# Clustered attention and two MLPs: idle products taken out, long GpSimd passes split or moved, fp32r transposes, last chunk in halves, a new order

## The chip, the cores and the metric

The kernel runs on one core of a Trainium2 chip. Five engines work side by side, each through its own queue in order: TensorE (PE in the rows, its weight loads PEld), VectorE (DVE), ScalarE (ACT), GpSimd (POOL), and SyncE (SP), which issues nearly all transfers. The metric is the device time in microseconds of one execution, as a median of several; less is better. A row of a trace names an engine, a line of the kernel (L746), the tiles that are written and read, and times in microseconds from the start of the span, unless ns is written.

## The reference

Cut to what matters. q, k and v are [2, 8, 768, 64], the centroids [8, 16, 64]; the weights arrive as fp64.

```python
q_assign = np.argmax(np.einsum('bhsd,hcd->bhsc', q_n, c_n), axis=-1)   # q_n, k_n, c_n: unit length
k_assign = np.argmax(np.einsum('bhsd,hcd->bhsc', k_n, c_n), axis=-1)
mask = q_assign[:, :, :, None] == k_assign[:, :, None, :]
scores = np.where(mask, scale * np.matmul(q, k.transpose(0, 1, 3, 2)), -1e9)
attn = softmax(scores)                                    # written out in the reference
x = np.matmul(attn, v)  ->  [B * S, H * D] = [1536, 512]
h = (x @ w1) * (x @ w2) @ w3                              # d_ff 1024
x = h @ w_out                                             # [1536, 512]
h = x @ w_in                                              # d_ff 2048
out = (h * np.clip(h + 3.0, 0.0, 6.0) / 6.0) @ w_out2     # [1536, 512]
```

## The kernel before

Every operand of a product is held as two fp32r parts, a high one (H, h, hi) and a low one (L, l, lo), and a product is made of three: high by high, high by low, low by high. The weights come as pairs of 32-bit words and are put together on the chip in steps c0 to c5 (ScalarE c0 and c2, GpSimd or VectorE c1 at L1008, VectorE c3 at L1017 and c5 at L1021).

**Attention** runs over 16 heads (batch by head), each with 768 queries and keys in six blocks of 128. For each head: two loads (lq, lk) into one tile qkn, query beside key (L585); six transposes on TensorE in two runs of three (T, L608, id_f is the fp32 identity), a high part on ScalarE (qkh, L615) and a low part on VectorE (qkl, L618); the products with the centroids (pa, L647, two halves by high and low); nine small steps oh0 to oh8 (L661 to L677) from the products to a code of each row's cluster; copies and transfers of codes and parts into the operands kk, qkH and qkL (Dk, Dq, Ck, Cq). Then for each of 96 (head, block) pairs: scores (S1 and S, pst, L746, 512 and 256 columns), row maximum (mx, L758, VectorE), exponential (ex, L780, ScalarE) into p; transposes of p in runs of four on id_r, the fp32r identity (pT, L796), a high and a low part of these (ph, pl), and the product with v (av, L820). A tile of p is made readable as fp32r by writing one unused column of it (praw, the value three, L769 and L771): that write is op pw, on any of ScalarE, VectorE and GpSimd.

**The first MLP.** w3 @ w_out is computed first: w3 is transposed on TensorE, in 16 runs of four (wt, L1040, id_f), and multiplied with w_out (w_mm, psw, L1068). x @ w1 and x @ w2 are made batch by batch (psab, L1144 and L1396), their product is g, and g by the combined weights gives x of the second MLP. From some 350 us on, the second batch and then the whole **second MLP** (psh L1707, po L1751, about 457 us to the end) run by a scheme with seven products where blocks would need eight; the sums and differences of its operands are made on VectorE, ScalarE and GpSimd, and each has its low part as a subtraction (L421 on GpSimd through sub_pool, L424 on VectorE through sub_dve). Names: Ll, Wl, gsl, xwl are low parts of weights and states, xs and xsum are sums of states. The twelve output chunks of 128 rows by 512 columns are copied by ScalarE (out_copy, tile osb) and stored by SyncE (out_store, L1761).

**Idle products** (idle_pe, L530 to L534, ops in L568 to L573): six places with 4, 2, 3, 5, 4 and 3 products of 128 by 512 on the identity, whose result nobody reads.

**What sets the order.** Every step is an op of a plan with an engine (or a choice of them), what it needs and which buffers it takes and gives back. The table RANK gives each op its place in one list of some 4,000, and ON the engine where there is a choice; Plan.order only verifies both. The list is emitted in this order, so each engine's queue is that list cut down to its ops.

Of the kernel before, what the change touches and what calls it, by code (L numbers as in the profile page):

```python
# [54 lines left out]
    "T": """  # L55
        17 19 27 38 143 145 275 280 426 429 562 563 699 701 814 819 935 938 1062 1068 1180 1190 1317 1319 1451 1452 1579 1585 1717
        1721 1853 1869""",
    "qkh": """
        20 24 31 42 164 175 286 288 436 438 568 570 703 706 823 826 942 948 1069 1072 1195 1201 1320 1323 1454 1457 1589 1595 1725
        1739 1863 1873""",  # L60
    "qkl": """
        23 26 36 49 171 193 291 299 439 451 577 579 713 721 830 832 955 954 1078 1077 1200 1205 1324 1328 1466 1461 1592 1603 1732
        1744 1881 1883""",
# [3 lines left out]
    "Ck": """  # L67
        72 71 152 149 268 272 384 389 541 547 667 660 793 797 931 925 1048 1043 1154 1157 1296 1288 1414 1410 1555 1542 1696 1690 1841
        1836 1943 1950""",
    "Cq": """  # L70
        74 77 144 168 263 279 379 394 538 616 664 707 788 806 918 967 1055 1067 1146 1168 1301 1305 1420 1448 1553 1624 1692 1756 1846
        1896 1936 1956""",
# [123 lines left out]
    "xdone": "2215",  # L196
    "Wh": "2106 2126 2136 2176",
    "Wl": "2113 2135 2150 2182",
    "top": "2203",
    "gsh": "2208 2211 2214 2220 2229 2227 2245 2293",  # L200
    "gsl": "2212 2218 2222 2226 2240 2246 2304 2311",
    "x2": """
# [174 lines left out]
def cluster_attention_moe_kernel(  # L377
# [14 lines left out]
    nc = tc.nc  # L392
# [42 lines left out]
    def blk(i):  # L435
        return slice(i * 128, i * 128 + 128)
# [1422 lines left out]
```

## Time and profile before

| | |
|---|---|
| time, median of 3 runs | 741.15 us (740.86 to 741.38) |
| the profiled execution | 741.47 us |
| its span | 739.7 us |
| TensorE busy | 719.0 us, 97% of the span |
| VectorE busy | 611.5 us, 83% |
| ScalarE busy | 546.8 us, 74% |
| GpSimd busy | 201.9 us, 27% |

The busy share of TensorE is taken over the whole span: 0 to 36 us is a start in which it waits for loads and for other engines, and after that it hardly stops. Matmuls are pipelined, so the duration of one is longer than what it adds to the queue; what one costs is read from the start of one to the start of the next. A wait is charged to the instruction that stands behind it, with the engine and tile that ended it.

### The profile page before, as it was taken

How to read it: one execution, taken by the hardware profiler on the slowest of the kernel's cores; microseconds unless marked ns; L12 is line 12 of the kernel's file. 1: busy time of each engine (PE TensorE's matmuls, PEld its weight loads, DVE VectorE, ACT ScalarE, POOL GpSimd, SP SyncE). 2: the span in 40 equal slices, each digit the busy share in tenths (PEclk: the TensorE clock that was granted, in tenths of full speed). 3: DMA queues.
4: the chain of work that ended last, by engine and by line, in shares of the span. 5: the costliest groups of instructions: out<-in, count | busy, mean ns of one | idle time of the engine just before them, and what ended most of it. 6: DMA issues, size and time to landing. Idle time of an engine off the chain costs nothing. (4 is left out here: it accounts for less than half of the span.)

```text
span 739.7 us, 12102 instructions
## 1 busy us (share of the span) xinstructions
PE 719.0 (97%) x4143; PEld 661.4 (89%) x4143; DVE 611.5 (83%) x1060; ACT 546.8 (74%) x1043; POOL 201.9 (27%) x258
## 2 busy tenths in 40 slices
PE   5699999999999999999999999999999999999998
PEld 4488888888999999999999999999888998998986
DVE  6999999999899888778999999888897666666542
ACT  4899999898888878789867676676666656564543
POOL 3452646332635263355301110110110210011100
PEclk9999999999999999999999999999999999999999
DMA  8668555465563656453566752633222221411202
GB/s 237 157 167 221 152 150 162 114 161 140 150 185 119 182 155 170 115 156 114 178 200 228 238 175 100 220 122 138 91 86 85 72 72 60 137 61 58 72 28 86
DMA packets 81742, 101.97 MB, mean 138 GB/s; under 512 B 30960, under 2 KB 56592, under 8 KB 81680
## 3 DMA queue, kind: packets, MB, share of 16 engines
q1 hardware_dynamic: 81680, 101.20, 45.7%
q8 instruction: 33, 0.54, 0.3%
q14 instruction: 29, 0.24, 0.1%
HBM read 71.34 MB, written 15.78 MB: 118 GB/s over the span
## 5 line engine op out<-in xcount | busy, mean ns | idle before, releaser
L424 DVE TENSOR_TENSOR pl<-ptr,ph 128x512 fp32r<-128x512 f32 x144 | 96.3, 681 | 7.3 <-ACT ph L427 6.9
L758 DVE TENSOR_REDUCE den<-pst 128x1 f32<-128x768 f32 x96 | 91.1, 949 | 10.3 <-PE pst L746 9.2
L427 ACT ACTIVATE ph<-ptr 128x512 fp32r<-128x512 f32 x144 | 84.4, 597 | 14.0 <-PE ptr L796 9.7
L780 ACT ACTIVATE p<-pst,den 128x768 f32<-128x768 f32 x96 | 86.8, 904 | 8.8 <-DVE den L758 7.5
L1144 PE MATMUL psab<-xT,abhl 128*128 128x384 f32 x384 | 81.2, 343 | 0.6 <-DVE g L1154 0.6
L1008 POOL TENSOR_SCALAR cvt<-cvt 128x512 f32<-128x512 f32 x55 | 39.3, 718 | 142.0 <-ACT cvt L427 110.3
L746 PE MATMUL pst<-kk,qkL 128*128 128x512 f32 (+1 forms) x192 | 71.4, 374 | 4.8 <-ACT p L780 4.7
L1144 PEld LDWEIGHTS psab<-xT,abhl 128*128 128x128 f32 x384 | 65.4, 188 | 2.0 <-DVE g L1154 0.9
L820 PE MATMUL av<-ph,vs 128*128 128x384 f32 x192 | 66.4, 346 | 0.0
L796 PEld LDWEIGHTS ptr<-id_r,praw 128*128 128x128 f32 x576 | 60.9, 140 | 5.8 <-DVE pl L424 0.2
L746 PE MATMUL pst<-kk,qkH 128*128 128x512 f32 (+1 forms) x192 | 64.2, 338 | 1.7 <-ACT qkH L427 1.3
L820 PE MATMUL av<-pl,vs 128*128 128x384 f32 x192 | 64.8, 338 | 0.0
L427 ACT ACTIVATE m_sn<-psh 128x384 f32<-128x384 f32 x64 | 31.3, 489 | 44.3 <-PE psh L1707 43.4
L796 PE MATMUL ptr<-id_r,praw 128*128 128x128 f32 x576 | 63.6, 240 | 0.0
L427 ACT ACTIVATE cvt<-raw 128x512 f32<-128x512 f32 x72 | 48.1, 672 | 11.8 <-DVE cvs L1021 6.8
L1017 DVE SCALAR_TENSOR_TENSOR cvs<-cvt,cvs 128x512 int32<-128x512 int32 x72 | 50.0, 696 | 7.5 <-POOL cvt L1008 4.2
L1021 DVE SCALAR_TENSOR_TENSOR cvs<-cvt,cvs 128x512 int32<-128x512 int32 x72 | 50.8, 709 | 0.4
L427 ACT ACTIVATE cvs<-raw 128x512 int32<-128x512 uint8 x72 | 48.1, 670 | 1.8 <-DMA set<-cvs 1.8
L1068 PE MATMUL psw<-woh,wT 128*128 128x512 f32 x128 | 49.3, 405 | 0.0
L746 PEld LDWEIGHTS pst<-kk,qkL 128*128 128x128 f32 x192 | 36.0, 187 | 12.2 <-ACT p L780 9.9
L1751 PE MATMUL po<-m_whl,m_gv 128*128 128x512 f32 x162 | 44.0, 393 | 0.0
L1729 ACT ACTIVATE tt<-m_sn,three 128x384 f32<-128x384 f32 x48 | 29.4, 613 | 18.8 <-DVE m_sn L1717 9.0
(198 smaller groups left out, 1836.0 us busy)
## 6 DMA issues: line engine op xcount, KB each, us to landing
raw<-in_moe_w_dram SPq DMA_DIRECT2D x32, 512.0 KB, 4.3
m_gb<-set SPq DMA_DIRECT2D x64, 256.0 KB, 2.9
raw<-in_moe_w_out_dram SPq DMA_DIRECT2D x24, 512.0 KB, 3.4
raw<-in_moe_w_in_dram SPq DMA_DIRECT2D x16, 512.0 KB, 4.9
set<-cvs SPq DMA_DIRECT2D x32, 256.0 KB, 3.0
kk<-qkH SPq DMA_DIRECT2D x16, 384.0 KB, 4.0
abp<-cvs SPq DMA_DIRECT2D x16, 256.0 KB, 2.8
b_gv<-abp SPq DMA_DIRECT2D x16, 256.0 KB, 4.7
```

The lines of the kernel that those rows point to most:

```text
L424: nc.vector.tensor_tensor(out=out, in0=a, in1=b, op=ALU.subtract)
L427: nc.scalar.activation(out=out, in_=in_, func=AF.Copy, **kw)
L746: x = mm(out=psr[:, t, ks_], lhsT=TT[nm, h][:, i, cs_], rhs=flat(TT["K", h][:, a])[:, ks_], start=st, stop=sp)
L758: done["mx", n] = [other_banks(nc.vector.tensor_reduce(out=den_at(h, 0, c), in_=psS[h, c], axis=AX.X, op=ALU.max, negate=True), ("S", n + 1))]
L780: done["ex", n] = [other_banks(nc.scalar.activation(out=p, in_=psS.pop((h, c)), func=AF.Exp, bias=den_at(h, 0, c), accum_out=den_at(h, 1, ...
L796: x = nc.tensor.transpose(pt[:, blk(j)], raw[h, hf][0][:, c, blk(kb)], id_r)
L820: mm(out=t[:, 0:HF], lhsT=vs_t[h][:, 2 * s + i, :], rhs=x_[:, c0:c0 + HF], start=(s == 0 and i == 0 and n == 0), stop=(s == 2 and i == 1 a ...
L1017: stt(out=s, in0=cvt[key], scalar=3, in1=s, op0=ALU.logical_shift_left, op1=ALU.bitwise_or)
L1021: stt(out=s, in0=cvt.pop(key), scalar=-0x80000000, in1=s, op0=ALU.bitwise_and, op1=ALU.bitwise_or)
L1068: mm(out=ps, lhsT=wT[m, hf][:, a, blk(kk)], rhs=w_[hf][:, kk, :], start=(kk == 0 and n == 0), stop=(kk == 3 and n == 2))
L1144: mm(out=ps[:, 0:HF], lhsT=s[:, w, a, blk(kk)], rhs=xT0[0][:, x_, kk, hf * HF:hf * HF + HF], start=(kk == 0 and n == 0), stop=(kk == KD - ...
L1751: mm(out=outs[b, c], lhsT=g[:, a, blk(c % 3)], rhs=w[:, w_, :], start=(first and a == 0 and w_ == 0), stop=(last and a == 1))
```

## The change

1. The six ops with idle products and idle_pe go.
2. sub_pool splits a pass of 512 columns and more in two halves. The ops Ll, Wl, gsl, xsum and xwl are fixed on VectorE, and xs too where it was a choice: from GpSimd to VectorE go two of Wl (1024 columns), five of Ll (512), three of xs (768) and one of xwl (768).
3. The transposes of queries and keys of heads 1 to 15 (90) and those of w3 (64) are done on id_r. The tile is read as fp32r, for which one column more is written first: new ops tw (15, one a head) and ww (16, one a run), on VectorE 4 and 4, on ScalarE 3 and 4, on GpSimd 8 and 8. The tiles qkn and cvs have 8 columns more and their buffers are named one by one (slots), and the load of a head's queries stands behind the last transposes of the head two before.
4. The last output chunk is copied in two halves, columns 0 to 255 by ScalarE and 256 to 511 by VectorE, and stored in two halves of 128 KB, the first from ScalarE's queue and the second from SyncE's.
5. RANK and ON are new throughout. Of the choices that both kernels have, c1 goes from GpSimd to VectorE 13 times and back 8 times, wol2 from VectorE to GpSimd 8 times and back 6 times; xh two and woh one move between ScalarE and GpSimd, Ck one from ScalarE to VectorE.

```diff
-    "idle": "48 85 101 148 41 61",
-    "lq": "0 1 62 156 297 185 446 611 849 970 1052 1221 1163 1322 1545 1618",
+    "lq": "0 6 66 162 196 340 541 587 740 892 1125 1120 1218 1359 1501 1621",
...
     def sub_pool(out, a, b):
-        nc.gpsimd.tensor_tensor(out=out, in0=a, in1=b, op=ALU.subtract)
+        n = out.shape[-1] // 2 if out.shape[-1] >= 512 else out.shape[-1]
+        for i in range(0, out.shape[-1], n):
+            x = (slice(None),) * (len(out.shape) - 1) + (slice(i, i + n),)
+            nc.gpsimd.tensor_tensor(out=out[x], in0=a[x], in1=b[x], op=ALU.subtract)
...
-    op(("idle", 0), "pe", 0.0, lambda: idle_pe(4), ("id",), due=-30, take=("a",), drop=("a",))
...
+    def pad_write(e, pad):
+        if e == "act":
+            return nc.scalar.activation(out=pad, in_=three, func=AF.Copy)
+        return (nc.gpsimd if e == "pool" else nc.vector).tensor_copy(out=pad, in_=three)
...
+    def qk_raw(e, h):
+        del q_n[h]
+        x = ar.tile([128, S + 8], F32R, tag=f"qkn{h % 2}", name="qkr")
+        qraw[h] = x[:, 0:S].rearrange("p (c d) -> p c d", c=NC), pad_write(e, x[:, S:S + 1])
+
     def qk_T(h, hf):
+        if h:
+            x, w = qraw.pop(h) if hf else qraw[h]
+            pt = ps_s.tile([128, HF], F32R, tag="s", name="ptqk")
+            W_["st", h, hf] = pt.bitcast(F32)
+            for c in range(3):
+                i = nc.tensor.transpose(pt[:, blk(c)], x[:, 3 * hf + c, :], id_r)
+                tc.add_manual_dep(i.ins, w.ins.name, SYNC)
+            return
...
+    def w3_raw(e, m, hf):
+        del cvo["w3", m, hf]
+        x = base.tile([128, 520], F32R, tag=f"cvs{held['w3', m, hf]}", name="cvr")
+        wraw[m, hf] = x, pad_write(e, x[:, 512:513])
...
     def w3_T(m, hf):
-        pt = W_["pt", m, hf] = ps_s.tile([128, 4, 128], F32, tag="s", name="pt")
+        x, w = wraw.pop((m, hf))
+        pt = ps_s.tile([128, 4, 128], F32R, tag="s", name="pt")
+        W_["pt", m, hf] = pt.bitcast(F32)
         for i in range(4):
-            nc.tensor.transpose(pt[:, i, :], cvo["w3", m, hf][:, blk(i)], id_f)
-        cvo.pop(("w3", m, hf))
+            j = nc.tensor.transpose(pt[:, i, :], x[:, blk(i)], id_r)
+            tc.add_manual_dep(j.ins, w.ins.name, SYNC)
+        give("w3", m, hf)
...
-        copy_act(t, outs[b, c], scale=1.0 / 6.0)
+        copy_act(t[:, 0:half_of(b, c)], outs[b, c][:, 0:half_of(b, c)], scale=1.0 / 6.0)
+
+    def half_of(b, c):
+        return 256 if (b, c) == (1, 2) else 512
+
+    def last_copy(b, c):
+        copy_on("dve", W_["osb", b, c][:, 256:512], outs[b, c][:, 256:512], scale=1.0 / 6.0)
+
+    def last_store(b, c, i):
+        r = slice(256 * i, 256 * i + 256)
+        (nc.sync if i else nc.scalar).dma_start(out=out[b * S:(b + 1) * S, :].rearrange("(p c) n -> p c n", c=NC)[:, c, r],
+                                                in_=W_["osb", b, c][:, r])
```

Three places show what the new table does. First SyncE at the start of the program, before (qkn holds queries and keys of a head, cen the centroids, raw weights, vn values):

```order
L585 DMA qkn<-in_q_dram 128x6x64 x2
L517 DMA cen<-in_centroids_dram 128x64
L989 DMA raw<-in_moe_w_dram 128x1024
L585 DMA qkn<-in_k_dram 128x6x64
L590 DMA vn<-in_v_dram 128x384
L585 DMA qkn<-in_k_dram 128x6x64
```

SyncE at the same place, after:

```order
L578 DMA qkn<-in_q_dram 128x6x64
L517 DMA cen<-in_centroids_dram 128x64
L1001 DMA raw<-in_moe_w_dram 128x1024
L578 DMA qkn<-in_k_dram 128x6x64
L578 DMA qkn<-in_q_dram 128x6x64
L578 DMA qkn<-in_k_dram 128x6x64
L583 DMA vn<-in_v_dram 128x384
```

The first head's keys are the fourth transfer and no longer the fifth; the second head's queries and keys follow, ahead of the values.

TensorE from the second head's second run of transposes to the first head's first scores, before (ptqk and pt are transposes, pa the assignment, pst scores):

```order
L608 MATMUL ptqk<-id_f,qkn 128x128 x3
L534 MATMUL idle<-id_r 128x512 x4
L1040 MATMUL pt<-id_f,cvs 128x128 x4
L534 MATMUL idle<-id_r 128x512 x4
L647 MATMUL pa<-qkH,cT 128x384
L647 MATMUL pa<-qkL,cT 128x384
L647 MATMUL pa<-qkH,cT 128x384
L647 MATMUL pa<-qkL,cT 128x384
L534 MATMUL idle<-id_r 128x512 x3
L746 MATMUL pst<-kk,qkL 128x512
L746 MATMUL pst<-kk,qkH 128x512
```

TensorE at the same place, after:

```order
L611 MATMUL ptqk<-id_r,qkr 128x128 x3
L1066 MATMUL pt<-id_r,cvr 128x128 x4
L657 MATMUL pa<-qkH,cT 128x384
L657 MATMUL pa<-qkL,cT 128x384
L657 MATMUL pa<-qkH,cT 128x384
L657 MATMUL pa<-qkL,cT 128x384
L758 MATMUL pst<-kk,qkL 128x512
L758 MATMUL pst<-kk,qkH 128x512
```

The eleven idle products are gone, the rest stands as it stood, and the transposes read the identity id_r and the retyped tiles qkr and cvr.

VectorE around the codes of the first head (ohs, then cd and the copy to kk) and the first step of the second head's assignment (as from pa), before:

```order
L618 SCALAR_TENSOR_TENSOR qkL<-ptqk,qks,qkH 128x384
L669 TENSOR_TENSOR as_240<-as_240,wtab 128x192
L1017 SCALAR_TENSOR_TENSOR cvs<-cvt,cvs 128x512
L665 TENSOR_REDUCE as_241<-as_240 128x12
L671 TENSOR_TENSOR ohs<-as_240,as_241 128x12x16
L661 STREAM_TRANSPOSE as_290<-pa 128x384
L677 STREAM_TRANSPOSE cd<-ohs 128x384
L468 CAST kk<-cd 16x384
```

VectorE at the same place, after:

```order
L675 TENSOR_REDUCE as_238<-as_237 128x12
L1034 SCALAR_TENSOR_TENSOR cvs<-cvt,cvs 128x512
L681 TENSOR_TENSOR ohs<-as_237,as_238 128x12x16
L1038 SCALAR_TENSOR_TENSOR cvs<-cvt,cvs 128x512
L628 SCALAR_TENSOR_TENSOR qkL<-ptqk,qks,qkH 128x384
L687 STREAM_TRANSPOSE cd<-ohs 128x384
L468 CAST kk<-cd 16x384 x2
L1034 SCALAR_TENSOR_TENSOR cvs<-cvt,cvs 128x512
L671 STREAM_TRANSPOSE as_296<-pa 128x384
```

The transpose of the codes (cd) stood behind the one that reads the second head's pa and now stands ahead of it; a step c5 and a low part qkL stand ahead of it instead, and the second copy to kk, which ScalarE made, is VectorE's.

## Rows read from the trace of the kernel before

**Rows 1.** Windows: busy us (instructions) of PE, PEld, DVE, ACT, POOL; clock; DMA.

```profile
345.00:460.00 115.00, 114.19 (x663) 112.93 (x661) 110.73 (x191) 84.95 (x150) 17.14 (x17) 1.00 0.59 190
460.00:740.00 280.00, 275.86 (x1391) 250.07 (x1389) 190.48 (x330) 165.47 (x301) 30.07 (x20) 1.00 0.27 92
```

**Rows 2.** Waits from 36 to 740 us: total us, times, longest.

```profile
PE psab L1144 <- DVE g L1154: 0.6, 1, 0.6
...
PEld pst L746 <- ACT p L780: 3.9, 13, 0.4
```

**Rows 3.** Timeline of SyncE's queue at the start: start, duration, line, transfer.

```profile
3.30 0.55 SPq L585 DMA_DIRECT2D qkn<-in_k_dram  x1
```

**Rows 4.** Timeline of TensorE to 36 us; in brackets, the wait and what ended it.

```profile
7.96 1.52 PE L608 MATMUL ptqk<-id_f,qkn 128*128 128x128 f32 x6 [7.96 <-DMA qkn<-in_k_dram]
...
12.75 0.52 PE L647 MATMUL pa<-qkL,cT 128*128 128x384 f32 x1
...
16.12 1.31 PE L534 MATMUL idle<-id_r 128*128 128x512 f32 x4
17.27 0.34 PE L647 MATMUL pa<-qkH,cT 128*128 128x384 f32 x1
...
20.36 0.50 PE L746 MATMUL pst<-kk,qkH 128*128 128x512 f32 x1 [1.30 <-ACT qkH L427]
...
33.90 1.41 PE L534 MATMUL idle<-id_r 128*128 128x512 f32 x5
```

**Rows 5.** Timeline of VectorE and ScalarE around the first scores.

```profile
18.16 0.58 DVE L661 STREAM_TRANSPOSE as<-pa 128x384 f32<-128x384 f32 x1 [0.92 <-PE pa L647]
18.67 0.54 DVE L677 STREAM_TRANSPOSE cd<-ohs 128x384 f32<-128x384 f32 x1
...
23.76 0.89 ACT L780 ACTIVATE p<-pst,den 128x768 f32<-128x768 f32 x1
```

**Rows 6.** Windows 17 to 36 us: all engines, then the idle products alone.

```profile
17.00:36.00 19.00, 12.79 (x69) 9.54 (x68) 16.51 (x30) 16.56 (x31) 8.38 (x11) 1.00 0.65 178
...
17.00:36.00 19.00, 4.17 (x15) 2.36 (x13) 1.00 0.65 178
```

**Rows 7.** Timeline of TensorE: a run of fp32r transposes, one of fp32.

```profile
43.09 0.46 PE L796 MATMUL ptr<-id_r,praw 128*128 128x128 f32 x4
43.38 0.47 PE L746 MATMUL pst<-kk,qkL 128*128 128x512 f32 x1
43.69 0.39 PE L746 MATMUL pst<-kk,qkH 128*128 128x512 f32 x1
43.92 0.34 PE L820 MATMUL av<-ph,vs 128*128 128x384 f32 x1
...
58.41 0.60 PE L1040 MATMUL pt<-id_f,cvs 128*128 128x128 f32 x4
58.76 0.42 PE L820 MATMUL av<-ph,vs 128*128 128x384 f32 x1
59.02 0.34 PE L820 MATMUL av<-pl,vs 128*128 128x384 f32 x1
59.20 0.33 PE L820 MATMUL av<-ph,vs 128*128 128x384 f32 x1
```

**Rows 8.** The pad writes of p: ns min/median/max, first and last start, forms.

```profile
L771 DVE CAST praw<-three x9: 111/154/154, 30.1 to 341.9; 128x1 fp32r<-128x1 f32 x9
```

**Rows 9.** One overlap (timeline); the conversion's and the subtraction's durations on VectorE (ns).

```profile
541.12 2.03 POOL L421 TENSOR_TENSOR x2f<-x2f 128x768 f32<-128x768 f32 x1 [10.49 <-ACT m_whl L427]
...
541.36 2.07 DVE L1008 TENSOR_SCALAR cvt<-cvt 128x512 f32<-128x512 f32 x1
...
L1008 DVE TENSOR_SCALAR cvt<-cvt x17: 412/421/2071, 68.4 to 541.4; 128x512 f32<-128x512 f32 x17
...
L424 DVE TENSOR_TENSOR m_w<-m_gb,m_w x11: 677/685/693, 468.1 to 710.0; 128x512 fp32r<-128x512 f32 x11
```

**Rows 10.** Timeline of ScalarE at the end.

```profile
736.10 0.60 ACT L427 ACTIVATE osb<-po 128x512 f32<-128x512 f32 x1 [2.17 <-PE po L1751]
```

More of the change, by code (lines that the diff above doesn't have):

```diff
@@ L215 @@
+    "abg": "1305 1393 1521 1556 1668 1705 1778 1828 1879 1944 2035 2092 2176 2210 2151 2286",
+    "xdone": "2240",
+    "Wh": "2133 2153 2166 2186",
+    "Wl": "2140 2168 2178 2202",
+    "top": "2227",
+    "gsh": "2232 2236 2239 2245 2249 2256 2292 2315",
+    "gsl": "2237 2243 2247 2251 2254 2294 2318 2337",
+    "x2": """
[5 rows of a table added]
+        2946 2948 2949""",
[6 rows of a table added]
     "bsm": """
-        2243 2283 2298 2315 2355 2367 2378 2390 2401 2412 2420 2422 2455 2457 2460 2461 2513 2530 2531 2537 2577 2581 2600 2618 2620
@@ L310 @@
+    "oc2": "3544 3546 3560 3563 3593 3598 4004 4010 4026 4013 4016 4023",
+    "os2": "3656 3621 3568 3860 3834 3852 4007 4021 4028 4019 4018 4025",
+    "oc3": "4027",
+    "os3": "4029",
 }
 ON = {
-    "Ck": "ad",
+    "Ck": "dd",
     "Cq": "aa",
-    "pw": "dppdppppaaapppppapdaddpaadaadpdd",
-    "oh1": "pppppppdppppppp",
+    "pw": "ppddadapdaapappapdadppapaadappaa",
+    "tw": "dppdpppapdaadpp",
+    "oh1": "ppppppppppppppd",
     "oh4": "ppppppppppppppp",
-    "xh": "apaa",
-    "c1": "ppppddpppppppppdppppppppppppppddpppppppppddpppddppppddpdpppppdppppdpdpdd",
@@ L320 @@
-    "woh": "appppppp",
-    "Wl": "ppdd",
-    "gsl": "dddddddd",
-    "bxl": "ddddddd",
-    "bxs": "dddd",
-    "g1s": "dddd",
-    "Ll": "dddddddddpdddddddpdddddpddpdddpd",
-    "wol2": "dddpdpddddddddppdpddddddpdddddpd",
-    "xwl": "dddddddddddddp",
-    "xs": "dpddpddp",
+    "xh": "appp",
+    "c1": "pppppdpppdpppppppppppppppppdpppppppddpddppdppdddddppddddpdpppdpppppdpddp",
+    "woh": "aapppppp",
+    "ww": "dppappdpppapddaa",
+    "wol2": "dpddpdddddddddpdddpppdddddppdddp",
 }
@@ L528, in cen_2 @@
         nc.scalar.activation(out=W_["cst"][:, 1:2], in_=W_["cst"][:, 0:1], func=AF.Sqrt)
-    def idle_pe(n):
-        t = ps_a.tile([128, 4, 128], F32, tag="a", name="idle")
-        for _ in range(n):
-            mm(out=t, lhsT=id_r, rhs=id_r.unsqueeze(1).to_broadcast([128, 4, 128]), start=True, stop=True)
     def cen_3():
@@ L583, in load_qk @@
         if i == 0:
-            q_n[h] = ar.tile([128, NC, 2 * D], F32, tag="qkn", name="qkn", bufs=2)
+            q_n[h] = ar.tile([128, S + 8], F32, tag=f"qkn{h % 2}", name="qkn")[:, 0:S].rearrange("p (c d) -> p c d", c=NC)
         nc.sync.dma_start(out=q_n[h][:, :, D * i:D * i + D], in_=src[b, hh].rearrange("(p c) d -> p c d", c=NC))
@@ L608, in qk_T @@
             nc.tensor.transpose(pt[:, blk(c)], q_n[h][:, 3 * hf + c, :], id_f)
+        if hf:
+            del q_n[h]
     def qk_hi(h, hf):
@@ L687, in prep_ops @@
         SB = {"p": 0.96, "d": 0.47}
-        op(("lq", h), "dma", 0.7, lambda: load_qk(q, 0, h), due=b - 12, lat=2.0, take=("qn",))
+        op(("lq", h), "dma", 0.7, lambda: load_qk(q, 0, h), due=b - 12, lat=2.0, take=("qn",), after=[("T", h - 2, 1)] * (h > 1))
         op(("lk", h), "dma", 0.7, lambda: load_qk(k, 1, h), [("lq", h)], due=b - 11.9, lat=2.0)
@@ L692, in prep_ops @@
         fop("s", ("vlo", h), SB if h >= WHOLE else {"p": 0.3}, lambda e: v_lo(e, h), (("vhi", h),), due=b - 1.9, drop=("vn",))
+        if h:
+            fop("tw", ("tw", h), {"a": 0.25, "p": 0.12, "d": 0.08}, lambda e: qk_raw(e, h), [("lq", h), ("lk", h)], due=b - 7, lock=False)
         for hf in range(2):
             dd = b - 6.5 + 0.4 * hf
-            op(("T", h, hf), "pe", 0.22, lambda hf=hf: qk_T(h, hf), [("lq", h), ("lk", h)], due=dd, take=("s",),
-               drop=("qn",) if hf else (), after=[("T", h, 0)] * hf)
+            op(("T", h, hf), "pe", 0.22, lambda hf=hf: qk_T(h, hf), [("tw", h)] if h else [("lq", h), ("lk", h)], due=dd, take=("s",),
+               drop=("qn",) if hf else (), after=[("T",) + divmod(2 * h + hf - 1, 2)] * (h + hf > 0))
             op(("qkh", h, hf), "act", 0.375, lambda hf=hf: qk_hi(h, hf), [("T", h, hf)] + [("qkh", h, 0)] * hf, due=dd + 0.05,
@@ L992, in cluster_attention_moe_kernel, with give @@
     ts, stt = nc.vector.tensor_scalar, nc.vector.scalar_tensor_tensor
+    slots, held = list(range(3)), {}
+    def give(*key):
+        slots.append(held.pop(key))
     def conv_ops(key, src, k_, due, big=None):
@@ L1011, in c_low @@
         def c_low(e):
-            s = cvo[key] = base.tile([128, 512], I32, tag="cvs", name="cvs", bufs=3)
+            held[key] = slots.pop(0)
+            s = cvo[key] = base.tile([128, 520], I32, tag=f"cvs{held[key]}", name="cvs")[:, 0:512]
             copy_act(s, raws.pop(key).bitcast(U8)[:, :, 3], scale=1.0 / 32.0, bias=-15.5 / 32.0)
@@ L1060, in wo_lo @@
         sub_on(e, wol[g // 4][:, g % 4, :], cvo.pop(("wo", g)), woh[g // 4][:, g % 4, :])
+        give("wo", g)
     def w_mm(m, g):
@@ L1130, in ab_lo @@
         sub_on(e, abs_[j][:, w, 1], cvo.pop(("ab", j, w)), abs_[j][:, w, 0])
+        give("ab", j, w)
     def ab_store(j, w):
@@ L1592, in set_store @@
         nc.sync.dma_start(out=set_dram[j][:, w], in_=cvo.pop(("set", j, w)))
+        give("set", j, w)
     for j in range(J2):
```

210 lines of the change are left out of this document (102 added, 108 removed), and 250 rows, old and new, of tables (RANK, RUN_ON).

## The prediction, made before the changed kernel was timed

> **What bounds the kernel now.** I read the windows first: TensorE is busy for 114.19 of the 115 us from 345 to 460 us, and for 275.86 of the 280 us from 460 to 740 us [rows 1]. VectorE stands at 110.73 of 115 us in the first of these stretches and at only 190.48 of 280 in the second. GpSimd has little to do in either (17.14 and 30.07 us). Then the waits after 36 us: TensorE's longest wait in its products is 0.6 us, once, for VectorE, and its weight loads wait 3.9 us in 13 pieces for the exponentials [rows 2]. So from 36 us to the end time goes down in two ways only: fewer nanoseconds of TensorE work, or fewer of those small waits. Ahead of 36 us it is otherwise: TensorE is busy for 12.79 of the 19 us from 17 to 36 us, and 4.17 of these are idle products, whose result nobody reads [rows 6]. There a chain sets the time: first loads, transposes, assignment, scores (L746), row maxima, exponentials.
>
> **The start.** SyncE issues the loads of queries of two heads before the centroids, and the first load of keys, which takes .55 us to issue, at 3.30 us [rows 3]; TensorE's first product waits for that load until 7.96 [rows 4]. The new order issues one load of queries fewer ahead of it, so the first transpose can come up to .55 us earlier, as long as the transfer itself takes as long as before. Next, four idle products stand at 16.12 ahead of the second assignment (17.27): 1.15 us [rows 4]. Behind that assignment VectorE waits .92 us for its result at 18.16, and the block of codes of the first head, which does not need it, is queued behind this wait (18.67) [rows 5]; from the codes come the copies and the transfers on which the scores at 20.36 wait 1.30 us [rows 4]. The new order of VectorE puts that block ahead of the second assignment's transpose, and the idle products are gone, so the first scores can come some 1.05 us earlier: the .92 us of the wait and a part of the issue time. Not all of it arrives at the exponential of 23.76 [rows 5], since ScalarE has conversions and a table load in front of it which are not earlier by as much; I take -.4 us of the 1.05. The idle products at 33.90 (1.41 us) stand ahead of scores [rows 4]; part of what they cost is caught up in later waits for an exponential, so I take -.8. The idle products between these two places fill waits for exponentials and cost nothing now. Start together: -1.2 us; the ends are -2.5 (1.15 + 1.41, all of it kept) and +.5 (the conversions are moved too, and if the first scores come behind one more product, that is the .50 of 20.36 [rows 4]).
>
> **The transposes.** I read them from start to start. A run of four fp32 transposes on id_f (L1040) goes from 58.41 to 58.76, .35 us, and the product behind it takes .26 to its successor (58.76 to 59.02), where the next of the same form takes .18 (59.02 to 59.20): .35 + .08. Four fp32r transposes on id_r (those of praw, L796, the same form as the new ones) go from 43.09 to 43.38, .29 us, and the product behind them takes .31 (to 43.69) where the next takes .23 (to 43.92): .29 + .08 [rows 7]. So a run of four saves .06 us and a run of three three quarters of that, .045. The change turns 64 transposes of w3 (16 runs of four) and 90 of queries and keys (30 runs of three) to fp32r. Of these, 14 and 28 runs lie behind 36 us: 14 x .06 + 28 x .045 = 2.1 us saved. Counted in the two orders, a run of transposes is followed by a product at 160 places now and at 153 before; each costs the .08 of above, so 7 x .08 = .6 us goes back. Net -1.5 us; bounds -2.1 (the extra places fall into waits) and -.5 (the fp32 runs lay beside waits that stay).
>
> The 31 pad writes, one column each, that let the tile be read as fp32r cost .154 us on VectorE [rows 8], and the row of ScalarE or GpSimd would be no more than .05 longer. Eight of them lie on VectorE: 1.2 us. Each puts one more step between a landed load and its transposes. Loads are issued several us ahead, so that step is hidden; where the cover fails (a head whose load lands late), the price is one pad write, .15 to .2 us. At the first heads there is no cover: .2 us, within the ends of the start.
>
> **Long passes on GpSimd.** At 541.12 GpSimd begins a 768-wide subtraction of 2.03 us, and at 541.36 VectorE a 512-wide conversion that takes 2.07 us, where the median of that form is .421 [rows 9]: both end nearly together, so VectorE stood still for 1.65 us. The change takes eleven such passes (512 to 1024 wide) to VectorE and cuts what stays in halves. But TensorE's waits for VectorE are few, .6 us the longest [rows 2], so the gain there is small: -.3 us, half of one such wait; the ends are 0 and -1.65, one stall of VectorE passed on whole. The Trainium skill, page "SBUF — State Buffer", section "Who interferes with whom", says that the engine which issues first holds the shared pair of ports for its whole instruction and the other one stands still; the trace agrees with 2.07 beside .421 us. By that rule halves bring the stall to half, not to nothing.
>
> The price is on VectorE. A 512-wide subtraction is .685 us there [rows 9], so the eleven passes (five of 512 columns, four of 768, two of 1024, together 7,680) come to 7,680 x .685 / 512 = 10.3 us by columns. All but the two 1024-wide ones (2.7 us, at 340 us) fall behind 460 us, where VectorE has 280 - 190.48 = 89.5 us free [rows 1]; the cover is ample and I cost them at nothing there; without it each would hold up its product by .7 us. In the attention part the conversions c1 (13 go from GpSimd to VectorE, 8 the other way) add 5 x .421 = 2.1 us, and the pad writes 1.2: 3.3 us to an engine that is 96% busy [rows 1]. I take a fifth of it as wait on TensorE, +.6; the ends are 0 and 2.2 (two thirds).
>
> **The last chunk.** ScalarE copies the last 512 columns in .60 us [rows 10]. After, ScalarE copies half, then VectorE the other half (it waits for the first in the new order), and two stores of half the size leave from two queues. Two halves one after the other take between .60 and 1.0 us with what each has fixed; the store is half as long. I take 0; ends -.4 and +.3.
>
> **The sum.** -1.2 - 1.5 - .3 + .6 + 0 = -2.4 us against the profiled execution's 741.47 (its span of 739.7 and 1.8 around it, which the change leaves alone): 739.1. The median of the runs is .3 us below that execution, so the forecast is 738.8 as a median.
>
> **The rivals.** *The clock (slower).* The assignment's products take .52 us at 12.75 and .34 at 17.27 [rows 4]: the first is the level of 1.2 GHz, the second 2.4 GHz, and between them TensorE ran without a gap, for a good part on idle products. Without these there are gaps, and TensorE may stay at 1.2 GHz till the work becomes dense at 36 us. Its real work from 17 to 36 us is 12.79 - 4.17 = 8.6 us [rows 6] and would take twice that; half of the extra hides in waits: +4.3 us on the sum: 738.8 + 4.3 = 743.1. It decides if the products at 17 us after the change still show about .5 us. Against it: a wait of 1.30 us before 20.36 did not take the clock down before. The Trainium skill, page "TensorE: Matmul & The Clock Gate", section "Part 4: PE-mode transpose", says that transposes do not count as busy for the clock in the way products do; no row here shows it, and by it the transposes that are left ahead of the second assignment would not raise the clock.
>
> *VectorE gives it back (no change).* All of the 3.3 us lies where it is 96% busy, and two thirds become waits of TensorE: 738.8 + 2.2 = 741.0. For it: the stretch from 345 to 460 us; against it: the waits for VectorE in rows 2 are few.
>
> *The new order takes the small waits too (faster).* Half of the 3.9 us in 13 pieces [rows 2] go: 738.8 - 2.0 = 736.8. For it: TensorE's order is set anew everywhere; against it: more turns from transposes to products.
>
> *The change does not do what it says:* the fp32r runs cost what the fp32 ones did, or a transfer lands late at a head's first scores and takes .5 to 2 us: 740.5 to 743.
>
> **How the numbers follow.** Differences of under .2% (1.48 us) can hardly be told from none here: faster is below 739.67, slower above 742.63. Forecast 50 in 100 (45 of them faster, 5 the same); VectorE gives it back 25 (24 same, 1 slower); clock 12 (all slower); small waits 10 (all faster); the last rival 3 (slower). Faster .55, same .29, slower .16. The range: the forecast's own terms by their ends give about 736 to 741; upwards it must reach past VectorE's 741.0 to the edge of the clock's case, 742.6, downwards to just below the 736.8 of the small waits, 736.0. What is left out is most of the clock's 12 and some 5 below.
>
> **What the new profile would show.** Right: the first transpose at about 7.4 us, assignment products of .34 us at 17 us, the first scores near 19.3, and dense work from about 35 us; steps of .29 us at every run of four and about .22 at every run of three; no conversion on VectorE beyond 1 us; waits on TensorE behind 36 us of under 3 us in sum. Wrong: products of .5 us behind 17 us; waits of TensorE for VectorE between 80 and 460 us; a scores product that waits for a transfer; fp32r runs whose next product starts as late as before.

## The result, and the profile after

The changed kernel takes 745.51 us (median of 5 runs, 744.81 to 745.63) where the kernel before, on the same chip, takes 741.38: ratio 1.0052, 95% interval 1.0041 to 1.0064. It is slower by about 4 us, where 2.4 us less were forecast, and above the range's upper end of 742.6. The profiled execution takes 745.4 us with a span of 743.6. All ratios here are taken without the few executions that ran much longer at a lower granted clock.

The windows of the changed kernel (columns as in rows 1; the second row answers rows 6, the last two rows 1):

```profile
0.00:17.00 17.00, 6.12 (x25) 5.04 (x25) 11.56 (x36) 7.03 (x13) 4.47 (x27) 1.00 0.77 201
17.00:36.00 19.00, 13.53 (x46) 9.69 (x47) 15.81 (x28) 15.93 (x30) 9.69 (x16) 1.00 0.84 241
...
345.00:460.00 115.00, 114.66 (x656) 113.15 (x656) 112.06 (x197) 82.60 (x147) 15.01 (x11) 1.00 0.62 198
460.00:740.00 280.00, 277.66 (x1392) 250.38 (x1390) 191.94 (x334) 167.39 (x301) 19.35 (x23) 1.00 0.27 87
```

TensorE is as busy as before (719.2 us in all, 719.0 before) although 21 products are gone and 154 transposes are shorter. In the last stretch it is busy for 277.66 of 280 us, with 1392 instructions where there were 1391 and 275.86 us. So either it does them more slowly or it does them later. Its start (timeline; it answers rows 4):

```profile
7.99 1.51 PE L616 MATMUL ptqk<-id_f,qkn 128*128 128x128 f32 x6 [7.99 <-DMA qkn<-in_k_dram]
...
12.84 0.52 PE L657 MATMUL pa<-qkL,cT 128*128 128x384 f32 x1
...
15.18 0.72 PE L1066 MATMUL pt<-id_r,cvr 128*128 128x128 f32 x4 [1.48 <-DVE cvr L572]
...
16.47 0.52 PE L657 MATMUL pa<-qkH,cT 128*128 128x384 f32 x1
18.20 0.69 PE L657 MATMUL pa<-qkL,cT 128*128 128x384 f32 x1 [1.21 <-DVE qkL L628]
...
24.79 0.58 PE L758 MATMUL pst<-kk,qkL 128*128 128x256 f32 x1 [2.62 <-ACT p L792]
...
28.33 0.63 PE L1096 MATMUL psw<-woh,wT 128*128 128x512 f32 x1
...
36.51 0.39 PE L1096 MATMUL psw<-woh,wT 128*128 128x512 f32 x1
```

The assignment's products still take .52 us at 16.47, and one of 512 columns .63 at 28.33 and .39 at 36.51: TensorE is at the 1.2 GHz level until 36 us, as the clock's rival had it. (The column of the granted clock reads 1.00 for these two windows all the same; here the level is read from the products.) And yet the scores at 24.79 start at the same time as in the kernel before, 24.79, since they wait 2.62 us for the first exponential. That one starts at 23.76 in both kernels [rows 5], behind a table load and conversions on ScalarE (timeline; first before, then after):

```profile
21.12 0.68 ACT L427 ACTIVATE cvt<-raw 128x512 f32<-128x512 f32 x1 [0.26 <-issue]
21.81 1.28 ACT L506 ACT_TABLE_LOAD   x1
```

```profile
21.25 1.28 ACT L506 ACT_TABLE_LOAD   x1
...
22.66 0.64 ACT L427 ACTIVATE cvt<-raw 128x512 f32<-128x512 f32 x1
23.21 0.65 ACT L427 ACTIVATE cvs<-raw 128x512 int32<-128x512 uint8 x1
23.76 0.88 ACT L792 ACTIVATE p<-pst,den 128x768 f32<-128x768 f32 x1
```

The table load comes .56 us earlier than before, but the conversion to cvt that stood ahead of it (21.12) now stands behind it (22.66) and takes these .55 us back.

The waits of TensorE from 36 to 740 us (it answers rows 2):

```profile
PE psh L1738 <- DVE m_sn L1748: 1.5, 1, 1.5
PE av L832 <- DVE pl L424: 1.0, 2, 0.7
PE psh L1738 <- ACT m_sn L427: 0.8, 1, 0.8
...
PEld pst L758 <- ACT p L792: 4.8, 13, 1.0
```

Two waits at psh, where the last MLP begins, are new: 1.5 and .8 us. Before the change TensorE did not wait there. The timeline of all engines from 478 to 496 us shows where they come from (m_gb holds fetched weights):

```profile
478.74 0.37 SPq L1640 DMA_DIRECT2D m_gb<-set  x1
...
479.23 1.22 DVE L424 TENSOR_TENSOR m_hl<-m_gb,m_hl 128x512 fp32r<-128x512 f32 x1
...
480.48 0.32 SPq L1657 DMA_DIRECT2D m_gb<-set  x1
480.86 0.42 SPq L1640 DMA_DIRECT2D m_gb<-set  x1
...
485.36 1.10 DVE L1645 TENSOR_TENSOR m_gb<-m_gb 128x256 f32<-128x256 f32 x3 [3.00 <-DMA m_gb<-set]
...
485.53 2.24 PE L1738 MATMUL psh<-m_x,m_gB 128*128 128x384 f32 x12
...
485.82 1.27 ACT L427 ACTIVATE m_gB<-m_gb 128x1280 fp32r<-128x1280 f32 x1 [3.46 <-DVE m_gb L1645]
...
488.04 0.47 ACT L427 ACTIVATE m_sn<-psh 128x384 f32<-128x384 f32 x1
...
488.21 2.14 POOL L421 TENSOR_TENSOR m_whl<-m_gb,m_whl 128x256 fp32r<-128x256 f32 x2 [6.14 <-ACT m_whl L427]
...
488.53 1.23 DVE L424 TENSOR_TENSOR m_w<-m_gb,m_w 128x512 fp32r<-128x512 f32 x1
...
491.42 1.31 PE L1738 MATMUL psh<-m_x1b,m_gB 128*128 128x384 f32 x6 [1.52 <-DVE m_sn L1748]
...
495.17 1.55 PE L1782 MATMUL po<-m_w,m_whl 128*128 128x512 f32 x6
```

Two halves of one set of weights (L1640) are fetched. Between them SyncE has another fetch (L1657), which may start only when VectorE's m_hl ends at 480.45; the second half stands behind it, goes out at 480.86 and not at 479.1, and VectorE can go on with it only at 485.36. VectorE waits 3.00 us for it and ScalarE 3.46 for VectorE; then the conversions of these weights stand ahead of the copy m_sn of the first results in ScalarE's queue (488.04) and of m_w and more in VectorE's, and TensorE, which waits for these copies, stands still for 2.3 us.

What the change was to bring at the transposes is there (timeline; it answers rows 7):

```profile
58.41 0.46 PE L1066 MATMUL pt<-id_r,cvr 128*128 128x128 f32 x4
58.70 0.47 PE L758 MATMUL pst<-kk,qkL 128*128 128x512 f32 x1
59.01 0.39 PE L758 MATMUL pst<-kk,qkH 128*128 128x512 f32 x1
```

A run of four goes from 58.41 to 58.70, .29 us, and the product behind it takes .31: as forecast.

### The profile page after: what moved, and what is told of

Read it like the earlier page. It is cut to its first block, busy times and chain, and to the rows that moved or that the text cites. A ratio compares the mean times of both kernels' runs of the same rounds, so it can differ in the third digit from the quotient of the medians.

```text
span 743.6 us, 12136 instructions
## 1 busy us (share of the span) xinstructions
PE 719.2 (97%) x4122; PEld 659.9 (89%) x4122; DVE 620.3 (83%) x1082; ACT 547.9 (74%) x1052; POOL 195.2 (26%) x292
## 5 line engine op out<-in xcount | busy, mean ns | idle before, releaser
L758 PE MATMUL pst<-kk,qkH 128*128 128x512 f32 (+1 forms) x192 | 66.1, 348 | 0.2 <-DVE kk L468 0.2
L1096 PE MATMUL psw<-woh,wT 128*128 128x512 f32 x128 | 51.3, 415 | 0.0
L1782 PE MATMUL po<-m_hl,m_gv 128*128 128x512 f32 x153 | 42.0, 393 | 0.0
```

The source lines that it names most:

```text
L758: x = mm(out=psr[:, t, ks_], lhsT=TT[nm, h][:, i, cs_], rhs=flat(TT["K", h][:, a])[:, ks_], start=st, stop=sp)
L1096: mm(out=ps, lhsT=wT[m, hf][:, a, blk(kk)], rhs=w_[hf][:, kk, :], start=(kk == 0 and n == 0), stop=(kk == 3 and n == 2))
L1782: mm(out=outs[b, c], lhsT=g[:, a, blk(c % 3)], rhs=w[:, w_, :], start=(first and a == 0 and w_ == 0), stop=(last and a == 1))
```

## The experiments

Behind the first measurement five chips were used, each with the kernel before beside it: one for e1 to e4, one for e5 to e8, one for a0 and e9 to e11, one for e12 to e15, one for e16 and e17. Between these groups the ratios are compared and not the medians. All medians, with the ratio to the kernel before there:

| run | median us | ratio, 95% interval |
|---|---|---|
| changed kernel, first measurement | 745.51 | 1.0052 (1.0041 to 1.0064) |
| a0_after | 743.56 | 1.0035 (1.0020 to 1.0050) |
| e1_idle_back | 743.76 | 1.0031 (1.0019 to 1.0043) |
| e2_no_idle | 741.14 | 0.9995 (0.9986 to 1.0004) |
| e3_fetch_first | 741.58 | 1.0002 (0.9993 to 1.0011) |
| e4_fp32 | 746.18 | 1.0059 (1.0045 to 1.0073) |
| e5_fetch_align | 741.43 | 1.0006 (0.9997 to 1.0014) |
| e6_before_shift | 743.47 | 1.0034 (1.0022 to 1.0046) |
| e7_fetch_align_idle | 740.58 | 0.9997 (0.9987 to 1.0006) |
| e8_fetch_align_fp32 | 742.57 | 1.0025 (1.0016 to 1.0035) |
| e9_fetch_place | 740.24 | 0.9980 (0.9972 to 0.9989) |
| e10_fetch_place_whole_passes | 742.45 | 1.0010 (1.0001 to 1.0019) |
| e11_fetch_place_idle | 740.06 | 0.9976 (0.9966 to 0.9985) |
| e12_before_place | 741.43 | 0.9997 (0.9988 to 1.0007) |
| e13_fetch_place_whole_last | 740.59 | 0.9987 (0.9978 to 0.9996) |
| e14_before_halves | 741.54 | 1.0003 (0.9994 to 1.0011) |
| e15_fetch_place_start_fp32 | 740.15 | 0.9983 (0.9971 to 0.9996) |
| e16_fetch_place_fp32 | 741.76 | 1.0000 (0.9991 to 1.0010) |
| e17_fetch_place_idle11 | 740.59 | 0.9990 (0.9981 to 1.0000) |

### The transfer behind a waiting one

e3: one place in RANK, the second half of the fetch (ff) ahead of the other fetch (wf); the four ops from wf on move back one place. The lists are cut at the dots:

```diff
     "ff": """
-        2839 2836 2924 2919 ...
+        2839 2836 2920 2919 ...
     "wf": """
-        2827 2829 2856 2931 2920 ...
+        2827 2829 2856 2931 2921 ...
```

> The changed kernel with one transfer moved: the second half of the second pair's weights for the last MLP (ff 1,0) is issued ahead of the fetch of an output weight (wf 4), which waits for VectorE, instead of behind it. Theory (a transfer behind a waiting one): the transfer that was issued at 480.9 us is issued at 479.1, VectorE's wait of 3.0 us at 485.4 shrinks to about 1.2, and of the 2.3 us for which TensorE waits at 488 to 491 us some 1.5 to 2 go: 743.6 to 744. Rival: the transfer itself is late because six others share the DMA engines, or TensorE waits for copies in ScalarE's queue anyway: less than .5 us faster.

Measured: 741.58, 3.9 us under the first measurement of the changed kernel. Timeline of the same place:

```profile
477.08 0.88 SPq L1640 DMA_DIRECT2D m_gb<-set  x2
...
480.90 1.10 DVE L1645 TENSOR_TENSOR m_gb<-m_gb 128x256 f32<-128x256 f32 x3 [0.19 <-DMA m_gb<-set]
...
483.88 2.24 PE L1738 MATMUL psh<-m_x,m_gB 128*128 128x384 f32 x12
...
485.95 2.25 PE L1738 MATMUL psh<-m_x1b,m_gB 128*128 128x384 f32 x12
...
490.65 1.56 PE L1782 MATMUL po<-m_w,m_whl 128*128 128x512 f32 x6
```

Both halves go out together, VectorE waits .19 us in place of 3.00, and psh runs without a wait. The 3.9 us are more than the 1.5 to 2 us of the theory. The changed kernel was run again, beside e9 to e11, to see what it takes there:

> The changed kernel unchanged, to stand beside the other runs of this call on one chip: 745 to 746, and TensorE waiting some 2 to 3 us for VectorE and ScalarE between 485 and 492 us.

It took 743.56, in twelve runs from 741.29 to 748.14, where e3 has 740.43 to 742.99. In its profile VectorE waits 2.59 us for the same transfer. What the transfer costs is read inside each trace, from the first product of psh to the first of po, the same 39 products of psh between them: 9.64 us in the changed kernel (485.53 to 495.17), 8.76 in a0, 8.31 in e1 below, and 6.77 in e3. So the late transfer costs 1.5 to 2.9 us, by when it happens to land. The rest of the 3.9 lies ahead of it: psh begins at 485.53 in the changed kernel's profile and at 483.88 in e3's, and .75 us of that stand already at the first exponential (23.76 and 23.01), which the edit cannot reach. In a0 the subtraction m_hl ahead of the transfer took .69 us and not 1.22, so it is the order in SyncE's queue that makes the wait, and GpSimd's pass beside m_hl only adds to it. Why the first measurement lies 2 us above a0 and so close together (744.81 to 745.63) is not shown.

### The clock and the idle products

e1, e7, e11 and e17 put idle products back: e1 into the changed kernel, e7, e11 and e17 into e5 and e9, which the next section explains. They stand at the first five of the six places of before, 16 of the 21 products (e17: 11, without the last two lines of the cut); the five that stood at 33.90 never come back. e2 takes all 21 out of the kernel before by issuing none.

```diff
@@ qk_T @@
+            if (h, hf) == (1, 1):
+                idle_pe(4)
@@ w3_T @@
+        if (m, hf) == (0, 0):
+            idle_pe(4)
@@ assign_mm @@
+        if h == 1:
+            idle_pe(3)
@@ scores @@
+        if n in (1, 2) and not part:
+            idle_pe(2 if n == 1 else 3)
```

> The changed kernel with 16 idle products put back at the five early places (4, 4, 3, 2 and 3, each 128 by 512), everything else as it is. Theory (clock): without idle products TensorE stays at 1.2 GHz until 36 us and the chain of scores and exponentials loses there; with them the second assignment's products take .34 us again, the scores at 33 us come about 1.4 us earlier, and the time falls by 1.0 to 2.0 us, to about 744. Rival (queue): the start is bound by loads, ScalarE and VectorE, so the idle products only take room in the queue: no change or up to 1 us slower, 745.5 to 746.5, whatever clock the products show.

> The kernel before with nothing changed but that its 21 idle products are not issued. Theory (clock): products stay at .52 us (384 columns) until the work is dense, and the time rises by 0.5 to 2.5 us, less than the slow clock alone costs because 2.4 us of idle products in the way of others are saved. Rival (the reckoning of the prediction): 1.0 to 1.2 us faster than before, because the places at 16.12 and 33.90 us are free.

> The kernel with the moved transfer and tiles of 528 columns, and with 16 idle products put back at the five early places. Theory (clock hidden): the first scores' products are at 2.4 GHz again, but the start is bound by loads and exponentials, so the time stays within .5 us of the kernel without idle products. Rival (clock): 1 to 2 us faster than that kernel, as the changed kernel was by 1.75 us with them.

> The same kernel (moved transfer, tiles in place, halves) with the 16 idle products at the five early places. Theory (start bound elsewhere): the first 36 us pass at 2.4 GHz and yet the work behind them comes at most .3 us sooner; within .4 us of the kernel without them. Rival (clock): .8 us or more faster, as the medians with tiles of 528 columns had it (740.58 against 741.43).

> The kernel with the moved transfer and tiles in place, with the 11 idle products at the first three places only (4 behind the second head's transposes, 4 behind the first of w3, 3 behind the second assignment) and none later. Theory (start bound by the exponentials): products of .34 us at 16 us and within .4 us of 740.2, whatever the clock does after 20 us. Rival (clock): it falls again behind 20 us without the later ones, and the time is that without idle products plus what they cost, 740.5 to 741.

The clock does what the rival said. Timeline of e11, the assignment's products of 16 us:

```profile
15.01 1.16 PE L572 MATMUL idle<-id_r 128*128 128x512 f32 x4
16.01 0.33 PE L664 MATMUL pa<-qkH,cT 128*128 128x384 f32 x1
...
24.18 0.38 PE L767 MATMUL pst<-kk,qkL 128*128 128x256 f32 x1 [3.27 <-ACT p L803]
```

.33 us, the 2.4 GHz level, where the changed kernel shows .52. But the scores still wait for the exponential, 3.27 us now, so what TensorE gains it waits off. e2 against before: nothing that can be told (741.14, interval across 1). e11 against e9 -.2 and e7 against e5 -.85, with intervals that overlap; e17, by its ratio, is .7 above e9, where the intervals overlap too. e1 came out 1.75 under the first measurement of the changed kernel, which is no proof of the clock: against a0 it is level, and its milestones at 357 us are those of the changed kernel (psx begins at 357.57 and 357.48). The number of e1 fits its theory and the cause does not: 1.3 us of the difference lies between psh and po (8.31 against 9.64), where the late transfer is. So no run shows that the 1.2 GHz of the start costs anything; the medians of e7 and e5 leave room for .9 us.

Nor did the idle products always keep the clock up. e12 and e14 below have them as in the kernel before, and their granted clock is .50 from about 25 to 32 us (512 columns in .63 us at 29.01 in e12), where the profile of the kernel before shows .40 at 29.25.

### Where the tiles lie

The change widens the three cvs tiles by 8 columns, 32 bytes each, so the tiles behind them move by 96 bytes. The tile of the weights Whl, later m_whl, is laid out from the other end and stays. Mean step of successive products with the same tiles, in ns from start to start:

| products, columns | before | e6 | changed | e5 | e9 |
|---|---|---|---|---|---|
| psx from gh and Whl, 384 | 173.3 | 176.6 | 176.8 | 174.3 | 173.6 |
| psab from b_x and b_L, 384 | 173.3 | 176.7 | 173.4 | 176.7 | 173.3 |
| po from m_hl and m_whl, 512 | 229.6 | 233.8 | 233.4 | 233.0 | 230.7 |
| psh from m_w and m_gB, 384 | 173.7 | 176.5 | 177.6 | 175.8 | 176.3 |

The first three rows agree within .6 ns in all other profiles with tiles in the same places. The last does not: in e14, where no tile is moved, it is 176.5, so it tells nothing of the place.

e6 makes this edit in the kernel before, and gives the output tiles that share these buffers the same width:

```diff
-            s = cvo[key] = base.tile([128, 512], I32, tag="cvs", name="cvs", bufs=3)
+            s = cvo[key] = base.tile([128, 520], I32, tag="cvs", name="cvs", bufs=3)[:, 0:512]
```

> The kernel before with nothing changed but the cvs tiles, 520 columns wide instead of 512 (the last 8 unused), which moves all tiles behind them by 96 bytes. Theory (address): products of psx step by 176.7 ns and no longer by 173.3, and with po and psh the time rises by 2 to 3 us: 743.5 to 744.5. Rival (order): no change, 741.5.

Measured 743.47, 2.2 us slower than before, with psx at the slow step. Timelines of TensorE; first before, then e6:

```profile
471.06 1.20 PE L1259 MATMUL psx<-gh1B,Whl 128*128 128x384 f32 x6
472.10 1.20 PE L1259 MATMUL psx<-gh1A,Whl 128*128 128x384 f32 x6
```

```profile
472.31 1.22 PE L1259 MATMUL psx<-gh1B,Whl 128*128 128x384 f32 x6
473.37 1.22 PE L1259 MATMUL psx<-gh1A,Whl 128*128 128x384 f32 x6
```

Six products go from 471.06 to 472.10, 173 ns each; after the move from 472.31 to 473.37, 177. No instruction differs but in its addresses. e12 widens the tiles of the kernel before to 640 columns, a move of 1536 bytes:

> The kernel before with cvs tiles of 640 columns instead of 512 (the rest unused): all tiles behind them move by 1536 bytes and stay at the same place within 512 bytes. Theory (placement): no change against before, within .5 us, where 520 columns cost 2.2 us; psx steps by 173.3 ns. Rival (any move or a longer tile costs): 1 to 2.5 us slower.

741.43: no change. So it is the place and not the width. In the changed kernel, e5 has 528 columns and e9 640 (and qkn tiles of 896), each with e3's order:

```diff
-            s = cvo[key] = base.tile([128, 520], I32, tag=f"cvs{held[key]}", name="cvs")[:, 0:512]
+            s = cvo[key] = base.tile([128, 640], I32, tag=f"cvs{held[key]}", name="cvs")[:, 0:512]
```

> The changed kernel with the transfer moved ahead as in the run with fetch_first, and with the three cvs tiles 528 columns wide instead of 520. 520 columns make each tile 32 bytes longer than the 512 of before, so that every tile behind them lies 96 bytes further and no longer at the same place within 64 bytes as the tile of the weights Whl and m_whl, which comes from the other end of the memory; with 528 it does again. Theory (address): products whose two operands lie differently within 64 bytes step more slowly (psx from Whl: 176.7 ns instead of 173.3 before; po from m_hl and m_whl: 233.4 instead of 229.6), and the step goes back with 528: 384 x 3.4 ns + 576 x 1.7 ns + some for psh and psab, together 2 to 3 us faster than with fetch_first alone, about 739.0. Rival: the slower steps come from the new order (other traffic of the memory at that time): within .5 us of fetch_first, 741.5.

> The changed kernel with the transfer moved ahead, with cvs tiles of 640 columns and qkn tiles of 896: every tile behind them lies again at the same place within 512 bytes as before the change (a tile of 528 columns had left it elsewhere: psx stepped by 174.0 ns, but psab from b_x by 176.7 and po from m_hl and m_whl by 233.0). Theory (placement): all groups step as before the change, psx by 173.3, psab from b_x by 173.3, po from m_hl and m_whl by 229.6 ns, which is 2 to 2.5 us less than with the moved transfer alone: about 739.3. Rival (order): the steps stay as they were, 741.5.

e5's theory fell: psx went back to 174, but psab from b_x rose to 176.7 and po stayed, and the time is that of e3 (741.43). That both operands lie alike within 64 bytes is not the rule; which distance is slow stays open. e9, meant to lie at the old places within 512 bytes, has the old steps for psx and psab and nearly so for po, and takes 740.24, below the kernel before. Its ratio and that of e3 differ by .0022, 1.6 us, with intervals that do not overlap; the 384 products of psx at 3.2 ns are 1.2 us of this by estimate. The two profiled executions differ by less (740.48 and 740.94): in e9 TensorE's products wait 1.2 us for VectorE and ScalarE at psab and psx where they wait .2 in e3, and what is left is .85 us behind the first po.

### What the parts are worth then

e4, e8 and e16 do the transposes in fp32 again (id_f, the same tiles, pad writes and order):

```diff
-                i = nc.tensor.transpose(pt[:, blk(c)], x[:, 3 * hf + c, :], id_r)
+                i = nc.tensor.transpose(pt[:, blk(c)], x[:, 3 * hf + c, :].bitcast(F32), id_f)
...
-            j = nc.tensor.transpose(pt[:, i, :], x[:, blk(i)], id_r)
+            j = nc.tensor.transpose(pt[:, i, :], x[:, blk(i)].bitcast(F32), id_f)
```

> The changed kernel with the transposes of queries, keys and w3 in fp32 again (identity id_f, same tiles, pad writes and order kept). Theory: runs of four take .36 instead of .30 us, runs of three .25 instead of .21, runs of six .61 instead of .46, and the product behind each is .014 later; behind 36 us that is 14 x .073 + 18 x .051 + 5 x .16 = 2.7 us: about 748.2. Rival: the transposes lie beside waits, and the change is under 1 us.

> The kernel with the moved transfer and tiles of 528 columns, transposes of queries, keys and w3 in fp32 again. Theory: with the wait at 485 us gone, what TensorE gains ahead of it counts, so fp32 costs its full 2.7 us here (about 3.3 with the products behind), where it cost .7 in the changed kernel: about 741.8. Rival: fp32r is worth less than 1 us because the transposes lie beside waits.

> The kernel with the moved transfer and tiles in place, with the transposes of queries, keys and w3 in fp32 again, in the same order and with the pad writes. Theory (saturated TensorE, no wait at 485 us to swallow it): 2.0 to 2.7 us slower than with fp32r (740.24), 742.2 to 742.9. Rival: 1.1 us, as the medians with tiles of 528 columns had it.

e16 is 1.5 us slower than e9 by its ratio as by its median, e8 1.1 slower than e5. Both are less than their theories had and more than their rivals. In the profiles psx begins 2.4 us later in e16 than in e9 and 1.8 later in e8 than in e5. e4 settles nothing: the changed kernel did not run on its chip and spreads by more than what is sought.

e10 undoes the halves in the new order, e14 puts them into the old one:

```diff
-        n = out.shape[-1] // 2 if out.shape[-1] >= 512 else out.shape[-1]
+        n = out.shape[-1]
```

> The same kernel (moved transfer, tiles in place) with GpSimd's subtractions undivided again. Theory: two halves of .74 us take GpSimd longer than a whole of 1.29 and stop VectorE twice, so the halves are worth nothing: within .4 us. Rival (the change's reason): halves let VectorE in between, and undoing them costs .5 to 1.5 us.

> The kernel before with nothing changed but sub_pool, which splits passes of 512 columns and more. Theory (an order fits the passes that it was made for): .5 to 1.5 us slower than before, as the new order lost 2.2 us when its halves were undone. Rival (halves free VectorE in any order): .5 to 2 us faster.

e10 is 2.2 us slower than e9, beyond what its theory and its rival allowed; e14 is level with before, which neither of its two theories had. A half takes GpSimd nearly .74 us and a whole 1.29 (durations on GpSimd in the changed kernel, then in the kernel before):

```profile
L421 POOL TENSOR_TENSOR wol<-cvs,woh x16: 718/739/752, 26.0 to 116.8; 128x256 fp32r<-128x256 f32 x16
```

```profile
L421 POOL TENSOR_TENSOR wol<-cvs,woh x8: 1283/1286/1294, 27.3 to 115.2; 128x512 fp32r<-128x512 f32 x8
```

So halves are worth nothing in the old order, and the new order loses without them. In e10 the longest new wait of TensorE is .5 us (for a pad write of p on VectorE), and its products' waits of .2 us and more behind 36 us come to 4.1 us, where e9 has 2.6; where the rest of the 2.2 comes from is not shown.

e13 does the last chunk whole, e15 the second head's transposes and the first of w3 in fp32 without their pad writes.

> The kernel with the moved transfer and tiles in place, with the last output chunk copied whole by ScalarE and stored whole by SyncE again. Theory (the prediction's): within .4 us of the kernel with halves, 740.2. Rival: the halves save a part of the last store, and the whole chunk is .5 to 1 us slower.

> The kernel with the moved transfer and tiles in place, with the second head's transposes and the first run of w3 in fp32 and without their pad writes, on which TensorE waited 1.17 and 1.48 us at 10.9 and 15.2 us. Theory (start bound by ScalarE's and VectorE's chain of exponentials): within .4 us, 740.2. Rival (pad writes cost the start): .5 to 1.2 us faster.

By their ratios e13 is .5 us above e9 and e15 .2, with intervals that overlap: no difference that can be told, as their theories had it. The waits of 1.17 and 1.48 us for pad writes at the start cost nothing, since the first exponential does not come from there: it begins 15.7 us behind the first transpose in e15 and 15.8 in e9.

e15 also shows the clock rising without an idle product. With these waits gone, and its transposes there fp32 and longer, its products of the second assignment take .34 us at 14.03; the granted clock is 1.00 from 14 us to 17.3 and, behind a wait of 2.79 us, .50 from 17.4 to 30.9. The time does not change with it.

## Why the prediction was wrong, point by point

**The transposes, -1.5: the mechanism right, the match of the number partly luck.** Runs of four step by .29 us and runs of three by .21, as forecast. But e16 undoes the saving alone, in the same order: it is the 2.1 of the sum that it measures, at 1.5 (e8: 1.1). The .6 that was to go back for more turns from transposes to products was undone by no run.

**The start, -1.2: not shown.** Its step "I take -.4 us of the 1.05" for the exponential of 23.76 gave 0 in the two profiles: the scores came earlier (19.53 for the product that began at 20.36 [rows 4]), but ScalarE's queue, with one conversion more behind its table load, held the exponential at 23.76. That the two times are equal is chance. The keys' load is issued at 2.61 and not at 3.30 us, and the first transpose comes at 7.1 to 7.9 us in the other profiles with this start, about the 7.4 forecast, where the starts of before have 8.0 to 8.1; the changed kernel's own profile is the late one with 7.99. The first exponential follows the first transpose by 15.7 to 16.0 us, so it comes at 22.9 to 23.8; with the start of before (its own profile, e6, e12, e14) it comes at 23.1 to 24.3. Some tenths of a gain are possible and cannot be told from the spread. The -.8 for the idle products at 33.90 stays unproven: taken out of the kernel before with all the others, they change nothing that can be told (e2), and there the slower clock comes with it.

**The clock's rival: the mechanism right, the price wrong.** TensorE stays at 1.2 GHz until 36 us. Half of 8.6 us was put on the path; by e7, e11 and e17 it is between nothing and .9, since TensorE waits longer for the exponentials than it loses. The result lies on this rival's side, but did not come about through it. The Trainium skill, page "TensorE: Matmul & The Clock Gate", section "Part 4: PE-mode transpose", has transposes not count for the clock in the way products do. The run of transposes at 15.18 did not raise it (.52 us at 16.47), and with idle products around it e11 shows .33, but that does not settle it: in e15 a stretch with fp32 transposes from 12.30 to 13.65 and no wait in it ends at the higher level, .34 us at 14.03. Waits for pad writes and transposes are not told apart here.

**Passes on GpSimd, -.3: mis-sized, and not of one size.** The halves are worth 0 in the old order (e14) and 2.2 us in the new one (e10), beyond the end of 1.65. No run takes the eleven moved passes back to GpSimd.

**VectorE gives back +.6: about right.** TensorE's waits for VectorE between 36 and 480 us are 1.2 us in sum (av 1.0, psab .2), where they were .8 before (.6 and .2); one of .7 lies between 100 and 200 us, where the prediction named such waits as a sign against it.

**The last chunk, 0: right**, as far as e13 can tell (.5 us in its favour, within the noise).

**What was missing.** First, "the cover is ample and I cost them at nothing there": behind 460 us VectorE has free time, but it is free because it waits, at 485 us for a transfer that stands in SyncE's queue behind a fetch which waits for VectorE. I walked the new order through SyncE's queue at the start only and not where the last MLP begins. That is 1.5 to 2.9 us. The last rival, a transfer that lands late, had the kind of thing, at 3 in 100, but at a head's first scores. Second, the tiles of 520 columns were told as part of the change and given no price. They are 1.3 to 1.6 us here (e9 against e3, by medians and by ratios) and 2.2 in the kernel before (e6). With both mended the changed kernel is at 740.24, 1.3 us below the kernel before, and with the early idle products at 740.06 (e11): that beats the kernel before by little, and a good half of the 2.4 us forecast is then there, though not from the terms of the sum one by one. The new order as a whole was not tried without the rest.

## What to carry to other kernels

When an order is set anew, walk each transfer queue at the place where one stage hands over to the next: a transfer that could go stands behind one that waits, and the engine that then idles looks in a table of busy shares like cover. Here a start that waited for ScalarE's chain hardly changed with TensorE's clock, so price such a clock by who waits for the product and not by the work. Read what an edit is worth inside the traces as well, from a milestone ahead of it to one behind it: a difference of medians can hold what the edit cannot reach. When a tile is made wider, compare the steps of a long run of products before and after, and pad to where the tiles lay.

## What the runs showed of the hardware that was not expected

The step between products depends on where their tiles lie in SBUF, with the same instructions: 173.3 ns against 176.6 for 384 columns, 229.6 against 233.8 for 512, and 2.2 us of 741 by a move of 96 bytes (e6), nothing by one of 1536 (e12). Which distance is slow was not settled: 96 bytes slow psx and 192 bytes hardly, while psab from b_x is slow in e5 and e6 and not in the changed kernel, whose tiles were widened by as much as e6's.
